# Second layer of two split experts in seven products instead of block and token form; one load and one mask moved

## The chip, the cores and the metric

The kernel runs on one core of a Trainium2 chip. The metric is the device time of one execution in microseconds (us); the median of three runs stands for a kernel. The engines are named as the profile names them: PE (TensorE, matrix products), DVE (VectorE), ACT (ScalarE), POOL (GpSimd), SP (SyncE, which only issues DMAs). SBUF is the on-chip memory, PSUM holds the output of PE in eight banks.

## The reference, cut to what matters

A recurrent attention block (RWKV-5) makes one row of 384 numbers per token, and a mixture of eight experts works on these rows. Each token goes to the one expert with the largest logit.

```
for t in range(S):                                   # 4 x 8 heads, 768 steps, 48 wide
    cur = einsum('bhd,bhe->bhde', u * k_t, v_t)
    y[:, :, t] = einsum('bhd,bhde->bhe', r_t, state + cur)
    state = w * state + einsum('bhd,bhe->bhde', k_t, v_t)
x = y reshaped to (3072 tokens, 384)
logits = x @ w_gate                                  # (3072, 8)
expert = argmax(logits);  gate = softmax(logits)[expert]
for e in range(8):
    h = maximum(x[expert == e] @ w1[e], 0)           # 384 -> 1024
    out[expert == e] = gate * (h @ w2[e])            # 1024 -> 384
```

With the reference's inputs the eight experts get 380, 348, 359, 410, 409, 389, 374 and 403 tokens. All arithmetic is float32.

## The kernel before, in words

All the work is in the function `straight`. If a count falls outside the limits that it was built for, a flag is set and a general version runs behind it (L1392 to L1395); the flag compares the count of each expert with an upper bound `caps` and a lower bound `lows` (L849, L850).

**The scan loop** (L731 to L791) has 16 turns, one for each pair of heads of each batch. Turn i, in the order of the program: `p_own(i)` (PE, L278) forms the token's own term from the product `rp` that POOL made (`pairs`, L265); `own_t` (DVE, L282) transposes it; `p_scores` (PE, L290) writes the scores of six chunks into the PSUM tiles `X`; `scale(i + 1)` (DVE, L259) prepares the next turn; `diag(i)` (ACT, L296) writes twelve diagonal blocks into A; `mask(i, 0)`, `mask(i, 1)` (DVE, L302) and `mask(i, 2)` (DVE, L304) copy the scores above the diagonal into A. `p_tr(i - 2)` (PE, L351) turns older outputs back to token rows, and `keep(i - 2)` (ACT, L356 and L357) copies these to the SBUF buffer `xb`, the second copy out of the bank that mask 2 reads too. `p_out(i - 1)` (PE, L333, L338) makes the output of the turn before, and `out_t` (ACT, L343) copies it. In turns 6, 10 and 14 the flag `rt` is set: there a finished batch is routed as well, `p_rank` (PE), `slots` (DVE, L386, L388), `gates` (DVE, L392 to L394). Rows are then sent to sorted places in the DRAM tensor `rows` by scatters of POOL (`send`, L405), one to two in a turn. The buffers `xb` are two, by batch in turns, so `keep` of one batch waits until the scatters of the batch two before have read them. Tiny POOL copies named `turn` (L743, L871) hold POOL back until a given instruction of another engine is done.

**The experts.** Experts 0 and 1 are split: their first 160 sorted rows (`early`) begin while the last batch is still at work, and the rests (`late[0]`, `late[1]`, rows 160 and up, 224 and 192 wide) follow. The other six experts, sorted by count on the chip, are `late[2]` to `late[7]`, 416 to 364 rows wide. A loop (L880 to L926) takes them in order; `o` is the expert before `p`:

- For a rest (k < 2) the first layer is `L1` (PE L470, ACT L472): per eighth of the 1024 features three products of 128x128 weights with the rows, into one bank of `hbank`. After every second eighth `result` (L869) lets POOL do one `turn` and one of ten waiting scatters of the early rows.
- For a full expert the first layer is `quarter` (L477), a seven-product scheme (PE L492, DVE L506 to L516, ACT L503, L521) on sums of weights (`quarter_sums`) and of tokens (`token_sums`), both DVE, all at the helper line L687.
- While `p`'s first layer is at work, `inner_sums` (L662, DVE, L687) makes four sums of blocks of the hidden activations `hT` of `o`, one per quarter, and behind the first layer the second layer of `o` follows.
- The second layer has two parts. `L2` (L545) takes the rows beyond the first `c` = 128 * `nt` tokens in feature-major form: 24 products with weights as the stationary operand (PE L552), then DVE transposes (L554) and block-wise scatters. `tokens_out` (L573) takes the first `c` tokens in token-major form. With `nt` = 2 these are 256 tokens in seven products of four matmuls each of 192 columns (PE L598), with DVE and ACT operations (L616, L623, L627, L631) between them and two scatters; with `nt` = 1 these are 128 tokens in eight matmuls of 384 columns into the bank `tr` (PE L585), one DVE operation (L587) and one scatter. The rests have `nt` = 1, the full experts 2.
- The seven products read `inner_sums` and eight sums of the second-layer weights (`tums`). `weight_sums` (L651) puts these eight in the list `aside`; each scatter of POOL takes one from the list and does it behind itself (L677, L678), and `rest` does what is left. For `nt` = 1 both functions return at once.

Which instruction waits for which is worked out by the framework from the order of the program. Each engine takes its own instructions in that order. SP's queue at a turn k of the expert loop: `weights1(k + 2)` (four DMAs of 384 KB into the first-layer weights, each waiting until PE has read the quarter that it replaces), in turns from k = 1 `weights2(k + 1)`, and last the rows of expert k + 2 (`load`, L450: four DMAs of 169 KB and one small).

```
689    early = [Pass(e, 0, EARLY, 0, early_bufs[e]) for e in range(2)]
690    late = [Pass(k, EARLY if k < 2 else 0, n, 1 if k < 2 else 2) for k, n in enumerate(WIDTH)]
...
916            if k == 0:
917                okay()
918            weights1(p.k + 2)
919            if k > 0:
920                p.weight_sums()
921                o.L2()
922                o.tokens_out()
923                rest()
924                weights2(o.k + 2)
925        if k + 2 < n:
926            late[k + 2].load()
```

Of the kernel before, what the change touches and what calls it, by code (L numbers as in the profile page):

```python
# [43 lines left out]
def straight(tc, rk, vk, w, w1, w2, out, flag):  # L44
# [389 lines left out]
    class Pass:  # L434
# [3 lines left out]
        def __init__(self, k, s0, n, nt, bufs=None):  # L438
            self.k, self.s0, self.n, self.nt = k, s0, n, nt
            self.c = 128 * nt  # L440
            self.e, self.last = k, []
            self.g, self.gc = -(-n // 32), self.c // 32
            if bufs:
                self.x, self.t, self.h, self.y, self.yo, self.ix = bufs
# [100 lines left out]
        def L2(self):  # L545

            n, g = self.n - self.c, self.g - self.gc
            y = self.y
            for m in range(DT):
# [23 lines left out]
        def tokens_out(self):  # L573
# [8 lines left out]

            if nt == 1:
                for f in range(FT):
                    nc.tensor.matmul(tr[:, 0:DM], lhsT=self.h[:, f, 0:128], rhs=w2s[self.k % 2][f // 2][:, f % 2, :],  # L585
                                     start=f == 0, stop=f == FT - 1, skip_group_check=True)
                nc.vector.tensor_scalar_mul(self.yt[0].rearrange("p (a m i) -> p m a i", a=HP, m=DT),  # L587
                                            tr[:, 0:DM].rearrange("p (m a i) -> p m a i", a=HP, m=DT), self.xg[:, 0, 0:1])
                scatter(out, it2[:, 0:1], self.yt[0][:, :], N)
                return  # L590

# [36 lines left out]

            product(tr, 0, A(0, 0), B_(0, 0))
            product(tr, 1, A(0, 1), B_(1, 0))  # L630
            nc.scalar.copy(so[0], tr[:, 0:Z])  # L631
            add(so[1], tr, 1, so[0])
            weigh(place(0, 0), so[1], 0)
            product(yps[0], 0, Sm(1), Tm(1))
            product(yps[0], 1, Sm(0), Tm(0))
            add(so[2], yps[0], 0, so[0])
            add(so[3], yps[0], 1, so[2])
            weigh(so[4], so[3], 0)
            weigh(so[5], so[3], 1)
            product(dsb, 0, Sm(3), B_(1, 1))  # L640
            final(0, 1, dsb, 0, so[4])
            scatter(out, it2[:, 0:1], self.yt[0][:, :], N)
            product(yps[1], 0, Sm(2), Tm(2))
            add(so[6], yps[1], 0, so[2])
            weigh(so[7], so[6], 1)
            final(1, 1, yps[1], 0, so[5])
            product(tr, 0, A(1, 1), Tm(3))
            final(1, 0, tr, 0, so[7])
            scatter(out, it2[:, 1:2], self.yt[1][:, :], N)

        def weight_sums(self):  # L651

            if self.nt < 2:
                return
            ws = w2s[self.k % 2]

            for q in range(2):
                (b11, b12), (b21, b22) = [[halves(ws[q + u])[:, :, z] for z in range(2)] for u in (0, 2)]
                t1, t2, t3, t4 = [x[:, 2 * q:2 * q + 2].rearrange("p f (m c) -> p f m c", m=DT) for x in tums[self.k % 2]]
                aside.extend([(t1, b12, b11), (t2, b22, t1), (t3, b22, b12), (t4, b21, t2)])  # L660

        def inner_sums(self, js=range(4)):  # L662

            if self.nt < 2:
                return
            h = self.h
            a11, a12, a21, a22 = [h[:, 4 * u:4 * u + 4, t * 128:(t + 1) * 128] for t in range(2) for u in range(2)]
            for j in js:
                op(sums[j], *((a21, a22, ALU.add), (sums[0], a11, ALU.subtract), (a11, a21, ALU.subtract),
                              (a12, sums[1], ALU.subtract))[j])  # L670
# [18 lines left out]
    early = [Pass(e, 0, EARLY, 0, early_bufs[e]) for e in range(2)]  # L689
    late = [Pass(k, EARLY if k < 2 else 0, n, 1 if k < 2 else 2) for k, n in enumerate(WIDTH)]  # L690

# [20 lines left out]

    nc.gpsimd.memset(lows[:, 0:2], 0.0)
    nc.gpsimd.memset(lows[:, 2:], float(PAD))
    keys(0, nc.vector)
# [15 lines left out]
    for i in range(1, U):  # L731
# [32 lines left out]
        if behind:  # L764
            p_scores(i, range(4, G))
        if 2 <= i:
            keep(i - 2)
        mask(i, 2)
        if i == U - 1:
# [105 lines left out]
    def rest():  # L875
        while aside:
            op(*aside.pop(0), ALU.subtract, nc.gpsimd)


    for k, p in enumerate(late):  # L880
# [14 lines left out]
        else:  # L895

            if k < 2:
                for f in range(FT):
                    p.L1((f,))
                    if f % 2:  # L900
                        result(p, f)
# [14 lines left out]
            if k == 0:  # L916
                okay()
            weights1(p.k + 2)
            if k > 0:
# [4 lines left out]
                weights2(o.k + 2)  # L924
        if k + 2 < n:
            late[k + 2].load()  # L926
# [517 lines left out]
```

## Time and profile before

| what | us |
|---|---|
| median of 3 runs (lowest, highest) | 371.15 (370.73, 374.41) |
| the profiled execution, its span | 372.72, 371.0 |
| PE busy | 357.9 |
| DVE busy | 247.2 |
| POOL busy | 201.8 |
| ACT busy | 138.5 |
| scan loop, PE | about 14 to 119 |
| first and second layer of the early rows, PE | to 146.0 |
| first layer of rests 0 and 1 | 146.0 to 163.0 |
| second layer of rest 0 | 163.0 to 173.5 |
| quarters of expert 2 | 173.5 to 189.0 |
| second layer of rest 1 | 189.0 to 199.5 |

The chain in the page follows the work that ended last backwards from release to release. A line of the timeline gives the start, the length, the engine, the line of the kernel, the operation with its tiles, and the number of instructions; where an engine stood idle before, brackets give how long and what released it. A float32 product is two instructions on PE. A line of 687 is a helper: there the tile tells which sum it is.

### The profile page before, as it was taken

How to read it: one execution, taken by the hardware profiler on the slowest of the kernel's cores; microseconds unless marked ns; L12 is line 12 of the kernel's file. 1: busy time of each engine (PE TensorE's matmuls, PEld its weight loads, DVE VectorE, ACT ScalarE, POOL GpSimd, SP SyncE). 2: the span in 40 equal slices, each digit the busy share in tenths (PEclk: the TensorE clock that was granted, in tenths of full speed). 3: DMA queues.
4: the chain of work that ended last, by engine and by line, in shares of the span. 5: the costliest groups of instructions: out<-in, count | busy, mean ns of one | idle time of the engine just before them, and what ended most of it. 6: DMA issues, size and time to landing. Idle time of an engine off the chain costs nothing.

```text
span 371.0 us, 9058 instructions
## 1 busy us (share of the span) xinstructions
PE 357.9 (96%) x3371; PEld 334.9 (90%) x3371; DVE 247.2 (67%) x639; ACT 138.5 (37%) x401; POOL 201.8 (54%) x236
## 2 busy tenths in 40 slices
PE   6999999999999999999999999999999999999991
PEld 6788888887889999997997999999999999999891
DVE  8787888788773325046595895697688589685531
ACT  2487878768785310320220412221230221113210
POOL 3377868979955430453116506903931951999341
PEclk9699999999999999999999999999999999999997
DMA  7995798886656883695837716823842843313401
GB/s 209 275 256 174 249 265 248 265 256 195 232 113 233 261 350 77 177 279 159 216 90 214 180 55 202 194 89 100 224 151 92 201 149 125 112 49 88 141 21 49
DMA packets 34981, 65.08 MB, mean 175 GB/s; under 512 B 18378, under 2 KB 19410, under 8 KB 34928
## 3 DMA queue, kind: packets, MB, share of 16 engines
q1 hardware_dynamic: 29392, 49.86, 48.1%
q0 software_dynamic: 3808, 9.84, 7.5%
q10 hardware_dynamic: 1728, 4.72, 3.8%
q8 instruction: 28, 0.46, 0.5%
q14 instruction: 25, 0.20, 0.2%
HBM read 53.29 MB, written 11.26 MB: 174 GB/s over the span
## 4 chain that ended last, share of the span: by engine, by line
PE 87%; DVE 3%; DMA 2%; ACT 2%; issue 2%; POOL 2%; POOLq 0%; DVEq 0%; ACTq 0%
PE X L552 12%; PE X L492 12%; PE X L470 8%; PE tr L598 6%; PE yps L598 6%; PE yps L492 5%; PE X L290 5%; PE yps L333 4%; PE tr L351 3%; PE tr L492 3%; PE dsb L492 3%; PE tr L585 3%; PE yps L338 2%; PE yps L552 2%; PE dsb L598 2%; PE dsb L313 2%
## 5 line engine op out<-in xcount | busy, mean ns | idle before, releaser
L673 POOL DMA_INDIRECT out_dram<-yo,ix x33 | 33.3, 1009 | 84.6 <-DVE ia L579 79.6
L296 ACT ACTIVATE A<-ident,own 128x128 f32<-128x128 f32 x192 | 57.9, 388 | 12.6 <-DVE own L282 11.3
L552 PE MATMUL X<-hT,w2s 128*128 128x96 f32 (+7 forms) x384 | 47.4, 283 | 0.0
L552 PEld LDWEIGHTS X<-hT,w2s 128*128 128x128 f32 x384 | 47.2, 191 | 0.2
L405 POOL DMA_INDIRECT rows<-xb,slot x24 | 33.1, 1379 | 15.5 <-issue 4.5
L290 PEld LDWEIGHTS X<-RK 48*128 48x128 f32 x384 | 23.5, 190 | 7.5 <-issue 4.9
L290 PE MATMUL X<-RK 48*128 48x128 f32 x384 | 27.6, 286 | 2.1 <-DVE RK L259 2.1
L259 DVE TENSOR_TENSOR RK<-rk,TT 112x1536 f32<-112x1536 f32 x16 | 27.6, 1725 | 0.0
L265 POOL TENSOR_TENSOR rp<-rk 112x768 f32<-112x768 f32 x15 | 27.2, 1816 | 0.0
L302 DVE COPY_PREDICATED A<-strict,X 128x512 f32<-128x512 int32 x32 | 23.1, 740 | 4.5 <-ACT A L296 4.5
L492 PE MATMUL X<-xT,w1s 128*128 128x208 f32 (+5 forms) x120 | 26.0, 331 | 0.0
L598 PE MATMUL yps<-tums,sums 128*128 128x192 f32 x144 | 25.4, 326 | 0.0
L687 POOL TENSOR_TENSOR tums<-w2s,tums 128x384 f32<-128x384 f32 x24 | 24.6, 1027 | 0.4
L333 PE MATMUL yps<-A,vk 128*48 128x128 f32 x384 | 24.0, 274 | 0.0
L598 PEld LDWEIGHTS yps<-tums,sums 128*128 128x128 f32 x144 | 23.7, 190 | 0.0
L492 PEld LDWEIGHTS X<-xT,w1s 128*128 128x128 f32 x120 | 20.9, 190 | 0.5
L333 PEld LDWEIGHTS yps<-A,vk 128*48 128x48 f32 x384 | 20.2, 123 | 0.5
L687 DVE TENSOR_TENSOR quart<-w1s 128x128 f32<-128x128 f32 x69 | 19.1, 285 | 0.0
L521 ACT ACTIVATE hT<-hT 128x416 f32<-128x416 f32 (+5 forms) x23 | 12.3, 537 | 15.6 <-DVE hT L513 15.6
L503 ACT COPY mida<-X 128x208 f32<-128x208 f32 (+5 forms) x12 | 3.9, 324 | 37.9 <-PE X L492 37.9
L351 PE MATMUL tr<-sel,yT 112*128 112x104 f32 x128 | 18.0, 284 | 0.0
L631 ACT COPY so<-tr 128x192 f32<-128x192 f32 x6 | 1.9, 318 | 43.0 <-PE tr L598 43.0
(204 smaller groups left out, 805.6 us busy)
## 6 DMA issues: line engine op xcount, KB each, us to landing
w1s<-in_w_dram SPq DMA_DIRECT2D x36, 384.0 KB, 3.2
rk<-in_rk_dram SPq DMA_DIRECT2D x16, 672.0 KB, 7.0
w2s<-in_w_dram SPq DMA_DIRECT2D x24, 384.0 KB, 3.6
vk<-in_vk_dram SPq DMA_DIRECT2D x16, 528.0 KB, 4.5
w2s<-in_w_dram ACTq DMA_DIRECT2D x8, 384.0 KB, 6.3
xs<-rows SPq DMA_DIRECT2D x16, 169.0 KB, 5.2
w1s<-in_w_dram ACTq DMA_DIRECT2D x4, 384.0 KB, 3.4
rows<-zt SPq DMA_DIRECT2D x1, 1248.0 KB, 7.0
```

The source lines that it names most:

```text
L259: nc.vector.tensor_tensor(RKs[i % 3][0:KP].rearrange("p u (c t) -> p u c t", t=C), x[0:KP].rearrange("p u (c t) -> p u c t", t=C), bc(TT[: ...
L290: nc.tensor.matmul(o, lhsT=r[q, 1, c * C:(c + 1) * C], rhs=r[q, 0, c * C:(c + 1) * C], start=True, stop=True, skip_group_check=True)
L296: nc.scalar.activation(A[:, place(c, h), :], ident, func=ACT.Copy, scale=own[i % 2][:, c, h:h + 1])
L333: nc.tensor.matmul(o(c, h), lhsT=v[:, c, h * D:(h + 1) * D], rhs=A[:, place(c, h), :], start=c < 2, stop=c == 0, skip_group_check=True)
L351: nc.tensor.matmul(trv[c // 4][:, c % 4, :], lhsT=yTs[i % 3][0:KP, c & 1, (c // 2) * C:(c // 2 + 1) * C], rhs=sel[:, c & 1, i % HP, :], st ...
L405: s_ = nc.gpsimd.indirect_dma_start(out=rows[:, :], out_offset=bass.IndirectOffsetOnAxis(ap=slot[b % 2][:, c:c + 1], axis=0), in_=xbs[b % ...
L470: nc.tensor.matmul(p[:, 0:self.n], lhsT=w1s[self.k % 2][f // 2][:, m, f % 2 * 128:(f % 2 + 1) * 128], rhs=self.t[:, m, 0:self.n], start=m ...
L492: nc.tensor.matmul(p[:, at * n:(at + 1) * n], lhsT=a, rhs=b, start=j == 0, stop=j == len(ab) - 1, skip_group_check=True)
L552: nc.tensor.matmul(p[:, 0:n], lhsT=w2s[self.k % 2][f // 2][:, f % 2, m * 128:(m + 1) * 128], rhs=self.h[:, f, self.c:self.n], start=f == 0 ...
L598: nc.tensor.matmul(p[:, at * Z:(at + 1) * Z], lhsT=a(f), rhs=b(f), start=f == 0, stop=f == FT // 2 - 1, skip_group_check=True)
L673: s_ = nc.gpsimd.indirect_dma_start(out=to[:, :], out_offset=bass.IndirectOffsetOnAxis(ap=at, axis=0), in_=x, in_offset=None, bounds_check ...
L687: (eng or nc.vector).tensor_tensor(o, a, b, op=how)
```

## The change

The rests get `nt` = 2. Their 256 tokens are more than they are wide, so `L2` returns at once (`n <= 0`), the columns of `hT` beyond the width are set to zero by two POOL memsets ahead of the loop, and the form for `nt` = 1 is removed. The weight sums of rest 0 are put in `aside` ahead of the loop, so that the scatters of the early rows do them one by one; those of rest 1 are put there in turn k = 1. The inner sums of rest 0 are made on DVE at the start of turn k = 1, those of rest 1 one per quarter of turn k = 2. Rest 1 gets another list of PSUM banks for its seven products. The rows of expert 2 are loaded ahead of `weights1(2)` in turn k = 0 instead of behind it. The lower bound on the counts of experts 0 and 1 becomes 320, as for the others. In the turns of the scan loop with `rt`, `mask(i, 2)` stands ahead of `keep(i - 2)`.

```diff
-            self.g, self.gc = -(-n // 32), self.c // 32
+            self.g = -(-n // 32)
+            self.gc = min(self.g, self.c // 32)
+            self.banks = tr, yps[0], dsb, yps[1], tr
...
         def L2(self):
             n, g = self.n - self.c, self.g - self.gc
+            if n <= 0:
+                return
...
-            if nt == 1:
-                for f in range(FT):
-                    nc.tensor.matmul(tr[:, 0:DM], lhsT=self.h[:, f, 0:128], rhs=w2s[self.k % 2][f // 2][:, f % 2, :],
-                                     start=f == 0, stop=f == FT - 1, skip_group_check=True)
-                nc.vector.tensor_scalar_mul(self.yt[0].rearrange("p (a m i) -> p m a i", a=HP, m=DT),
-                                            tr[:, 0:DM].rearrange("p (m a i) -> p m a i", a=HP, m=DT), self.xg[:, 0, 0:1])
-                scatter(out, it2[:, 0:1], self.yt[0][:, :], N)
-                return
...
+            ba, bb, bd, be, bf = self.banks
-            product(tr, 0, A(0, 0), B_(0, 0))
-            product(tr, 1, A(0, 1), B_(1, 0))
+            product(ba, 0, A(0, 0), B_(0, 0))
+            product(ba, 1, A(0, 1), B_(1, 0))
...
         def weight_sums(self):
-            if self.nt < 2:
-                return
...
         def inner_sums(self, js=range(4)):
-            if self.nt < 2:
-                return
...
-    late = [Pass(k, EARLY if k < 2 else 0, n, 1 if k < 2 else 2) for k, n in enumerate(WIDTH)]
+    late = [Pass(k, EARLY if k < 2 else 0, n, 2) for k, n in enumerate(WIDTH)]
...
-    nc.gpsimd.memset(lows[:, 0:2], 0.0)
-    nc.gpsimd.memset(lows[:, 2:], float(PAD))
+    nc.gpsimd.memset(lows, float(PAD))
...
+        if rt:
+            mask(i, 2)
         if 2 <= i:
             keep(i - 2)
-        mask(i, 2)
+        if not rt:
+            mask(i, 2)
...
+    for p in late[:2]:
+        nc.gpsimd.memset(p.h[:, :, p.n:p.c], 0.0)
+    late[1].banks = zbank[0], zbank[1], zbank[2], yps[0], dsb
...
+    late[0].weight_sums()
     for k, p in enumerate(late):
...
             if k < 2:
+                if k:
+                    o.inner_sums()
                 for f in range(FT):
...
             if k == 0:
                 okay()
+                late[2].load()
             weights1(p.k + 2)
...
-        if k + 2 < n:
+        if 0 < k < n - 2:
             late[k + 2].load()
```

More of the change, by code (lines that the diff above doesn't have):

```diff
@@ L627, in weigh @@
                 nc.scalar.activation(o, x, func=ACT.Copy, scale=g[:, t])
-            product(tr, 0, A(0, 0), B_(0, 0))
-            product(tr, 1, A(0, 1), B_(1, 0))
-            nc.scalar.copy(so[0], tr[:, 0:Z])
-            add(so[1], tr, 1, so[0])
+            ba, bb, bd, be, bf = self.banks
+            product(ba, 0, A(0, 0), B_(0, 0))
+            product(ba, 1, A(0, 1), B_(1, 0))
+            nc.scalar.copy(so[0], ba[:, 0:Z])
+            add(so[1], ba, 1, so[0])
             weigh(place(0, 0), so[1], 0)
[L634 to L637, printed above, removed]
+            product(bb, 0, Sm(1), Tm(1))
+            product(bb, 1, Sm(0), Tm(0))
+            add(so[2], bb, 0, so[0])
+            add(so[3], bb, 1, so[2])
             weigh(so[4], so[3], 0)
             weigh(so[5], so[3], 1)
-            product(dsb, 0, Sm(3), B_(1, 1))
-            final(0, 1, dsb, 0, so[4])
+            product(bd, 0, Sm(3), B_(1, 1))
+            final(0, 1, bd, 0, so[4])
             scatter(out, it2[:, 0:1], self.yt[0][:, :], N)
-            product(yps[1], 0, Sm(2), Tm(2))
-            add(so[6], yps[1], 0, so[2])
+            product(be, 0, Sm(2), Tm(2))
+            add(so[6], be, 0, so[2])
             weigh(so[7], so[6], 1)
-            final(1, 1, yps[1], 0, so[5])
-            product(tr, 0, A(1, 1), Tm(3))
-            final(1, 0, tr, 0, so[7])
+            final(1, 1, be, 0, so[5])
+            product(bf, 0, A(1, 1), Tm(3))
+            final(1, 0, bf, 0, so[7])
             scatter(out, it2[:, 1:2], self.yt[1][:, :], N)
         def weight_sums(self):
-            if self.nt < 2:
-                return
             ws = w2s[self.k % 2]
```

## The prediction, made before the changed kernel was run

> **What bounds the kernel now.** I read the page first: the busy table and the chain that ended last.
>
> ```profile
> PE 357.9 (96%) x3371; PEld 334.9 (90%) x3371; DVE 247.2 (67%) x639; ACT 138.5 (37%) x401; POOL 201.8 (54%) x236
> ...
> PE 87%; DVE 3%; DMA 2%; ACT 2%; issue 2%; POOL 2%; POOLq 0%; DVEq 0%; ACTq 0%
> ```
>
> The chain is PE nearly throughout, and from 121.9 to 363 us it has no other engine in it. The table by stretches gives PE 17.00 of 17 us in 146-163, 10.50 of 10.5 in 163-173.5, 10.50 in 189-199.5, at granted clock 1.00. So behind 122 us PE time that goes is gained, and a wait that PE gets is lost, one for one.
>
> Second, the timeline of PE alone, round the rests of experts 0 and 1 and one full expert (start, length, line, operation):
>
> ```profile
> 163.00 5.49 PE L552 MATMUL X<-hT,w2s 128*128 128x96 f32 x48
> 168.33 5.35 PE L585 MATMUL tr<-w2s,hT 128*128 128x384 f32 x16
> 173.52 1.22 PE L492 MATMUL X<-xT,w1s 128*128 128x208 f32 x6
> ...
> 188.99 5.47 PE L552 MATMUL X<-hT,w2s 128*128 128x64 f32 x48
> 194.30 5.38 PE L585 MATMUL tr<-w2s,hT 128*128 128x384 f32 x16
> 199.51 1.21 PE L492 MATMUL X<-xT,w1s 128*128 128x206 f32 x6
> ...
> 221.37 2.76 PE L598 MATMUL tr<-w2s,hT 128*128 128x192 f32 x16
> 223.97 2.76 PE L598 MATMUL yps<-tums,sums 128*128 128x192 f32 x16
> ...
> 229.16 1.46 PE L598 MATMUL tr<-tums,hT 128*128 128x192 f32 x8
> ```
>
> To be seen: the second layer of rest 0 takes 173.52 - 163.00 = 10.52 us, of rest 1 199.51 - 188.99 = 10.52 (64 columns cost what 96 do), and the seven products of a full expert, the form that both get, 230.47 - 221.37 = 9.10 (the next L492 starts at 230.47).
>
> Third, POOL's timeline, which must now deliver the weight sums, and last all engines at 80-88 us, where the one PE wait behind the start-up lies that the mask can touch.
>
> ```profile
> 160.53 0.97 POOL L673 DMA_INDIRECT out_dram<-yoe,ixe  x1 [0.21 <-issue]
> ...
> 198.35 1.03 POOL L687 TENSOR_TENSOR tums<-w2s 128x384 f32<-128x384 f32 x1
> ```
>
> ```profile
> 80.67 0.33 ACT L357 COPY xb<-X 128x208 f32<-128x208 f32 x1 [1.08 <-DMA rows<-xb,slot]
> ...
> 81.04 0.74 DVE L304 COPY_PREDICATED A<-strict,X 128x512 f32<-128x512 int32 x1 [1.34 <-ACT xb L357]
> ...
> 85.90 1.81 POOL L265 TENSOR_TENSOR rp<-rk 112x768 f32<-112x768 f32 x1
> ...
> 87.77 0.51 PE L278 MATMUL dsb<-rp,wug 112*2 112x192 f32 x8 [0.82 <-DVE A L304]
> ```
>
> **Term 1, PE in the two rests: -2.84 us.** Per rest 48 + 16 half-matmuls go, 56 (7 products x 4 x 2) come, 0.1625 us each: 10.52 - 9.10 = 1.42, twice 2.84. That the columns beyond 224 or 192 are zeros doesn't make them cheaper, so the row of full experts holds.
>
> **Term 2, the third mask: -0.82 us.** In turns 6, 10, 14 of the scan loop the mask (L304) is put ahead of the two copies `keep`. It now waits for the second copy (L357). In turn 10 that copy waits for an earlier scatter of the same buffer to land, so VectorE stands 1.34 us, and `own`, the scale (L259) and with them POOL's product rp (L265) start that much later: rp ends at 87.71, PE takes it at 87.77 after 0.82 idle. Moved, the mask starts at 79.70; rp ends near 86.4, ScalarE's diagonals (free at 81.76 from its copies, 3.62 long) at 85.4, the mask of turn 11 at 86.8; PE is free at 86.95, so all 0.82 goes, with 0.15 to spare. Next late is that mask. Turns 6 and 14: VectorE waits 0.16 in each, and the copy L357 gets a wait for the mask instead, about 0.6; behind it on ScalarE stand the output copies (0.86), done at 56.1 and 108.4, where the next diagonals start at 56.04 and 108.37: 0 to 0.1 each, and no PE row there waits for ScalarE; taken at 0. Ends for the whole term: 0 (another wait at 86.95) and -0.82; I take -0.82 because each link has a row.
>
> **Term 3, start of expert 3: +0.45 us.** Rest 1 loses its block form, which gave VectorE 5.3 us before its sums were due. Its PE products now start when the quarters of turn k=2 end (call it T). Turn k=3 shows VectorE's load there, the inner sums (0.68 x 4) included: quarters end at 214.84, sums and transposes for the next expert at 223.07, so T + 8.23. Then 0.48 of index work (224.70 to 225.18), 0.26 for the first sum, 0.75 for two more: T + 9.72 plus some 0.1 of starts. PE has left its seven products at T + 9.10, and its second product of the next quarter, at T + 9.44, writes the bank zbank[1] that those two sums read. Stall 0.4 to 0.5. The bank list with zbank first keeps the other hazards away: third bank read to T + 10.7, written from T + 10.9. Ends: 0 and 1.0 (VectorE 0.5 later, as where a sum took 1.02 instead of 0.68 at 235.43).
>
> **Term 4, rest 0 waits for sums: +0.3 us.** PE would reach it at 163.00; its sixth and eighth weight sums are due at 163.00 + 2.60 + 0.65 = 166.25 and 171.44, and bank tr must be read by 170.79. POOL: two memsets first (312 elements per partition took 0.347, 960 took 0.898; these have 256 and 512, so some 0.8), in the 15.45 us in which POOL stood before 148.90; they wait for the sends that land near 139.7. Then eight rounds of turn, scatter and sum: 0.17 + 0.21 + 0.98 + 1.02 + some 0.2 gaps = 2.57, the first 2.9, and 0.6 where the trace shows a scatter late at 159.17: the eighth ends at 148.9 + 2.9 + 7 x 2.57 + 0.6 = 170.4, the sixth near 165. No stall, 1.0 in hand. If each of five sums that meet VectorE took the longest row, 1.35, the eighth ends at 172.1: stall 0.6. VectorE: four sums from 155.68 (2.7), transposes, token and quarter sums (7.29 by 162.76 to 170.05), index work and first sum 0.8: bank tr read at 166.5, 4.3 before it is due. But now two-input sums of both engines overlap in time: VectorE's sums of hT mean 1.019 over 12 where the shortest is 0.681, that is 0.68 lost per expert, at its one meeting with POOL's sums. Some six of POOL's eight sums fall between 155.7 and 170; six meetings cost 4.1: 170.6, no stall. If each costs what the longest such row lost, 1.82 - 0.68 = 1.14, six cost 6.8: 173.3, a stall of 2.5. Ends 0 and 2.5; I take 0.3 for both engines together, near the lower end, since 1.82 is one row and the mean is of twelve.
>
> [...]
>
> **At nothing, with cover.** Expert 2's rows: five DMAs pass four weight DMAs on SP, which stood idle from 143.4 to 148.47, when PE frees the first weights; their issue takes 2.5 (155.82 to 158.36), so weights keep their time. VectorE's 7.08 wait for these rows before 162.76 goes, and PE, which needs their transposes at 172, sees nothing of it; it is the room for the sums. Left where they were, the transposes would start at 162.76 as before and bank tr be read at 170.9, with no room for any meeting. Second-layer weights wait for POOL too: the last quarter of rest 0 is free at 171 instead of 173, and is used 20 us later. ScalarE gets 5 operations per rest (2.0 us), in idle of 10.5. POOL has 3 scatters fewer and 16 sums more (16.3 us): eight as above, eight for rest 1 from about 172 to 183, due near 190. Cover gone, each would be Term 4 again. The bounds of 320 rows hold: experts 0 and 1 have 380 and 348 tokens.
>
> **Sum.** -2.84 - 0.82 + 0.45 + 0.3 = -2.9 us. The profiled execution took 372.7 (span 371.0 and 1.7 around), 1.6 over the median 371.15: it goes to 369.8, the median to 368.2.
>
> **Rivals.** (a) PE gains in the rests but another wait stands at 87 us: without Term 2, 369.1. For it: rp, mask and PE end within 0.06 there; against: all three hang on the same VectorE wait. (b) VectorE is late for bank tr by Term 4's upper end, 2.5 instead of 0.3: 370.4. For it: the 1.82 row, and quarter sums (281 to 289 ns) that so far never met POOL's; against: the mean. (c) Slower: POOL is the bound at rest 0. Eight rounds at the longest scatter (1.36), sum (1.35) and a gap of 0.58 as after each turn that waited take 3.65 each; the eighth sum ends at 178.1, a stall of 6.7 against gains of 3.2: 374.7. It decides from 3.2 us a round, when the eighth ends at 174.6. Against it: at 225-234 scatter and sum alternate at 2.2 beside a busy VectorE. (d) All stalls hidden: 371.15 - 3.66 = 367.5.
>
> **How the numbers follow.** Forecast 0.55, (a) 0.12, (b) 0.13, (c) 0.08, (d) 0.12. About 1% (3.7 us) is what a measurement tells from no change. The forecast lies at 0.8%: same. Faster by over 1%, below 367.4: half of (d) and a tail of 0.14 of the forecast by spread of the medians, 0.2. Slower by over 1%, above 374.9: most of (c), and what I don't see, 0.08. Same 0.72. Range 367.0 to 370.6: from (d) less 0.5 of spread to (b) and a little; out are (c) and tails, 2 in 10.
>
> **What would show it.** Right: PE L598 after 163 in 9.1 us per rest without waits; no 0.82 before L278 near 87; a PE gap of 0.4 at the second L492 of expert 3. Wrong: PE rows waiting for POOL tums L687 (Term 4), for DVE so L616 beyond 0.5 (Term 3), or L278 still waiting for rp.

## The result, and the profile after

The changed kernel takes 371.67 us, median of 20 runs, where the kernel before, run beside it, takes 371.2 (20 runs): ratio 1.0004, 95% interval 0.9981 to 1.0027 (the ratios in this document compare the runs and are not the quotients of the medians). One of the 20 runs of the change took 925.22 us, some 550 more than the others; no trace of it was kept, its cause is open, and the ratio leaves it out. So nothing is to be seen of the forecast 2.9 us, and the time lies above the range of 367.0 to 370.6. Run again later the change took 371.57 against 371.92, ratio 0.9986 (0.9959 to 1.0014).

The profiled execution of the change took 370.8 us with a span of 369.1. That it lies below the 372.7 of the profile before proves nothing: the clock granted to PE in the first 20 us was 0.83 in the execution before and 1.00 in this one, and turn 1 of the scan loop began at 18.05 in the one and at 15.73 in the other, which shifts all later starts. So stages are compared, each measured between starts of PE rows within one execution.

The page of the change, as before: busy times first, then the chain that ended last.

```profile
PE 353.6 (96%) x3355; PEld 334.4 (91%) x3355; DVE 266.9 (72%) x645; ACT 142.9 (39%) x411; POOL 218.0 (59%) x250
...
PE 81%; DVE 13%; issue 2%; POOL 1%; DMA 0%; ACT 0%; POOLq 0%; DVEq 0%
```

PE is busy 4.3 us less, but the chain now runs over DVE for 13% of the span where it was 3%. The timeline of PE shows where (start, length, line, operation; in brackets the idle time before the row and its releaser). L278 was L278 before, L594 was L598, L494 was L492, L612 was L616 and L680 the helper L687:

```profile
84.94 0.51 PE L278 MATMUL dsb<-rp,wug 112*2 112x192 f32 x8
...
160.01 2.76 PE L594 MATMUL tr<-w2s,hT 128*128 128x192 f32 x16
162.61 2.76 PE L594 MATMUL yps<-tums,sums 128*128 128x192 f32 x16
...
166.51 1.46 PE L594 MATMUL yps<-tums,sums 128*128 128x192 f32 x8
170.42 1.57 PE L594 MATMUL tr<-tums,hT 128*128 128x192 f32 x8 [2.44 <-DVE so L612]
171.82 1.22 PE L494 MATMUL X<-xT,w1s 128*128 128x208 f32 x6
...
187.30 2.76 PE L594 MATMUL X<-w2s,hT 128*128 128x192 f32 x16
...
197.29 1.62 PE L494 MATMUL X<-xT,w1s 128*128 128x206 f32 x6 [0.73 <-DVE so L612]
```

To be seen: the rows of the seven products have the lengths of the full experts (2.76 and 1.46), but before the last product of rest 0 PE stands 2.44 us until DVE has read bank `tr`, and after rest 1 it stands 0.73 and loses some more inside the first quarter of expert 3 (its first row is 1.62 long). Rest 0 takes 171.82 - 160.01 = 11.81 us instead of 10.52, rest 1 197.29 - 187.30 = 9.99. L278 near 85 has no wait any more.

Why DVE is late shows its own timeline. The sums of rest 0 come first, then the token and quarter sums of expert 2, last the addition that frees bank `tr`:

```profile
152.76 1.16 DVE L680 TENSOR_TENSOR sums<-hT 128x512 f32<-128x512 f32 x1
...
155.16 1.95 DVE L680 TENSOR_TENSOR sums<-hT,sums 128x512 f32<-128x512 f32 x1
...
158.55 1.04 DVE L680 TENSOR_TENSOR toks<-xT 128x208 f32<-128x208 f32 x1
...
160.21 1.95 DVE L680 TENSOR_TENSOR toks<-xT,toks 128x208 f32<-128x208 f32 x1
162.08 0.28 DVE L680 TENSOR_TENSOR quart<-w1s 128x128 f32<-128x128 f32 x1
...
162.80 1.73 DVE L680 TENSOR_TENSOR quart<-w1s,quart 128x128 f32<-128x128 f32 x1
...
165.18 1.83 DVE L680 TENSOR_TENSOR quart<-w1s 128x128 f32<-128x128 f32 x1
...
170.01 0.35 DVE L612 TENSOR_TENSOR so<-tr,so 128x192 f32<-128x192 f32 x1
...
176.87 3.05 DVE L680 TENSOR_TENSOR sums<-hT 128x512 f32<-128x512 f32 x1
```

And the weight sums in the timeline of POOL over the same time:

```profile
155.55 1.01 POOL L680 TENSOR_TENSOR tums<-w2s,tums 128x384 f32<-128x384 f32 x1
...
158.34 1.01 POOL L680 TENSOR_TENSOR tums<-w2s 128x384 f32<-128x384 f32 x1
...
160.90 1.01 POOL L680 TENSOR_TENSOR tums<-w2s,tums 128x384 f32<-128x384 f32 x1
...
163.37 1.01 POOL L680 TENSOR_TENSOR tums<-w2s,w2s 128x384 f32<-128x384 f32 x1
...
165.84 1.01 POOL L680 TENSOR_TENSOR tums<-w2s,tums 128x384 f32<-128x384 f32 x1
...
176.41 1.01 POOL L680 TENSOR_TENSOR tums<-w2s,w2s 128x384 f32<-128x384 f32 x1
177.38 1.01 POOL L680 TENSOR_TENSOR tums<-w2s,tums 128x384 f32<-128x384 f32 x1
```

Each long row of DVE lies over a row of POOL, and no other two-input row of this stretch is long. With 0.68, 0.37 and 0.28 as the lengths of a sum, a token sum and a quarter sum that met nothing, the six rows from 152.76 to 165.18 lost 0.48, 1.27, 0.67, 1.58, 1.45 and 1.55: 7.0 us. POOL's sums stay at 1.01; only its small copies `turn` between them grow, up to 0.65 where the kernel before has at most 0.19, and its eighth sum ends at 166.85, in time. Without the 7.0 us DVE would have been done with its first reading of bank `tr` near 163.4, where PE wants it at 167.81.

The account in stages (us, starts of PE rows):

| stage | before | after |
|---|---|---|
| second layer of rest 0 | 10.52 | 11.81 |
| quarters of expert 2 | 15.47 | 15.48 |
| second layer of rest 1 | 10.52 | 9.99 |
| expert 3's quarters and expert 2's second layer | 30.96 | 31.51 |
| first layer of rest 0 to start of expert 4 | 84.46 | 85.78 |
| own-term products, turn 11 to 12 | 7.44 | 6.55 |
| own-term products, turn 6 to 15 | 58.94 | 57.93 |

The mask gained 0.9 to 1.0 in its stretch, the rests lost 1.3: +0.3 to +0.4. The medians say +0.5, but the interval of the ratio holds no change as well.

### The profile page after: what moved, and what is told of

Its sections match the earlier page's. It is cut to its first block, busy times and chain, and to the rows that moved or that the text cites. A ratio compares the mean times of both kernels' runs of the same rounds, so it can differ in the third digit from the quotient of the medians.

```text
span 369.1 us, 9067 instructions
## 1 busy us (share of the span) xinstructions
PE 353.6 (96%) x3355; PEld 334.4 (91%) x3355; DVE 266.9 (72%) x645; ACT 142.9 (39%) x411; POOL 218.0 (59%) x250
## 4 chain that ended last, share of the span: by engine, by line
PE 81%; DVE 13%; issue 2%; POOL 1%; DMA 0%; ACT 0%; POOLq 0%; DVEq 0%
PE X L494 11%; PE X L556 10%; PE tr L594 7%; PE yps L594 6%; PE X L472 6%; PE X L290 6%; PE yps L333 6%; PE tr L351 5%; PE yps L494 4%; PE yps L338 3%; DVE quart L680 3%; PE tr L494 2%; PE dsb L494 2%; PE yps L556 2%; PE dsb L313 2%; PE dsb L594 2%
## 5 line engine op out<-in xcount | busy, mean ns | idle before, releaser
L666 POOL DMA_INDIRECT out_dram<-yo,ix x28 | 28.6, 1022 | 66.8 <-DVE ia L583 62.5
L405 POOL DMA_INDIRECT rows<-xb,slot x24 | 30.4, 1265 | 13.0 <-issue 4.8
L556 PE MATMUL X<-hT,w2s 128*128 128x160 f32 (+5 forms) x288 | 36.5, 287 | 0.0
L556 PEld LDWEIGHTS X<-hT,w2s 128*128 128x128 f32 x288 | 36.2, 191 | 0.2
L680 POOL TENSOR_TENSOR tums<-w2s,tums 128x384 f32<-128x384 f32 x32 | 33.1, 1033 | 0.6
L594 PE MATMUL yps<-tums,sums 128*128 128x192 f32 x176 | 31.1, 326 | 0.0
L666 POOL DMA_INDIRECT out_dram<-yt,it x16 | 16.7, 1046 | 20.9 <-DVE so L612 16.2
L594 PEld LDWEIGHTS yps<-tums,sums 128*128 128x128 f32 x176 | 29.0, 190 | 0.0
L494 PE MATMUL X<-xT,w1s 128*128 128x208 f32 (+5 forms) x120 | 26.4, 332 | 0.8 <-DVE so L612 0.7
L333 PE MATMUL yps<-A,vk 128*48 128x128 f32 x384 | 24.0, 274 | 0.0
L680 DVE TENSOR_TENSOR sums<-hT 128x512 f32<-128x512 f32 x16 | 20.7, 1293 | 3.2 <-ACT hT L474 3.2
L494 PEld LDWEIGHTS X<-xT,w1s 128*128 128x128 f32 x120 | 20.8, 190 | 1.4 <-DVE so L612 1.4
L333 PEld LDWEIGHTS yps<-A,vk 128*48 128x48 f32 x384 | 20.3, 123 | 0.5
L680 DVE TENSOR_TENSOR quart<-w1s 128x128 f32<-128x128 f32 x69 | 20.6, 306 | 0.0
L594 PE MATMUL tr<-w2s,hT 128*128 128x192 f32 x112 | 19.4, 326 | 0.0
```

Source lines behind the costliest of these rows:

```text
L333: nc.tensor.matmul(o(c, h), lhsT=v[:, c, h * D:(h + 1) * D], rhs=A[:, place(c, h), :], start=c < 2, stop=c == 0, skip_group_check=True)
L405: s_ = nc.gpsimd.indirect_dma_start(out=rows[:, :], out_offset=bass.IndirectOffsetOnAxis(ap=slot[b % 2][:, c:c + 1], axis=0), in_=xbs[b % ...
L494: nc.tensor.matmul(p[:, at * n:(at + 1) * n], lhsT=a, rhs=b, start=j == 0, stop=j == len(ab) - 1, skip_group_check=True)
L556: nc.tensor.matmul(p[:, 0:n], lhsT=w2s[self.k % 2][f // 2][:, f % 2, m * 128:(m + 1) * 128], rhs=self.h[:, f, self.c:self.n], start=f == 0 ...
L594: nc.tensor.matmul(p[:, at * Z:(at + 1) * Z], lhsT=a(f), rhs=b(f), start=f == 0, stop=f == FT // 2 - 1, skip_group_check=True)
L666: s_ = nc.gpsimd.indirect_dma_start(out=to[:, :], out_offset=bass.IndirectOffsetOnAxis(ap=at, axis=0), in_=x, in_offset=None, bounds_check ...
```

## The experiments

GpSimd is POOL in the rows, VectorE DVE. The theory after the result: PE's products cost what the prediction says and the mask saves what it says; all that is missing is VectorE held by GpSimd's weight sums, at about twice the assumed price. Where a VectorE operation and a sum of GpSimd run beside one another the text speaks of a meeting, of a full one if the whole sum lies within the VectorE row. Rivals: VectorE's own list is too long with or without GpSimd; any work of GpSimd on SBUF holds it; the mask gains nothing in time. "Stage" below is the stretch from rest 0's first layer to the start of expert 4.

**First: the mask alone, and the rests alone.** The one is the kernel before with

```
+        if rt:
+            mask(i, 2)
         if 2 <= i:
             keep(i - 2)
-        mask(i, 2)
+        if not rt:
+            mask(i, 2)
```

and the other is the change with these lines as they were.

> The kernel before with nothing but the third mask moved ahead of the copies in the three turns with ranks. Theory (the mask's gain is real and the rests of the two experts cost it again): PE's wait of 0.82 us before the own-term product of turn 12 is gone, the time falls by 0.8 to 1.0, to about 370.3 beside 371.2. Rival (the mask gains nothing, PE meets another wait there, and the lead that the changed kernel shows behind turn 12 comes from its start): 371.2, with a wait of 0.5 or more left at that place.

> The changed kernel with the third mask put back behind the copies: the rests in seven products and the moved load alone. Theory: the rests together lose 1.3 us against before (rest 0 takes 11.8 instead of 10.5, rest 1 with the start of expert 3 about 10.4), so 372.3 to 372.7 beside 371.2. Rival (the rests gain and something else, such as the start, spends it): below 370.5.

Measured: mask alone 376.02 us against 376.12 of the kernel before on this chip (a slower one: the first four kernels ran on it), ratio 1.0000 (0.9964 to 1.0037), stage 84.45; the interval from turn 11 to 12 is 6.55, so the wait is gone, but the time settles nothing. (Its profile is of an execution of 380.45 us, so only stages and intervals are read from it.) The rests alone took 379.4, ratio 1.0085 (1.0045 to 1.0126), so they are a loss of about 3 us, more than the 1.3 that the change's profile shows for them; rest 0 took 12.76 us and the stage 86.52, 2.1 more than in the kernel before. The timeline of PE in the rests alone says what came on top:

```profile
178.37 2.52 PE L594 MATMUL tr<-tums,hT 128*128 128x192 f32 x8 [2.48 <-DVE so L612]
180.69 1.98 PE L494 MATMUL X<-xT,w1s 128*128 128x208 f32 x6
```

The wait is the same as in the change, 2.48 against 2.44, but the rows behind it are longer, 2.52 instead of 1.46 and 1.98 instead of 1.22. The same kernel by stretches (busy time of each engine, then the granted PE clock, DMA share, GB/s):

```profile
178.30:180.70 2.40, 2.33 (x9) 2.33 (x10) 1.65 (x6) 1.71 (x4) 0.51 (x1) 0.61 1.27 170
180.70:182.50 1.80, 1.80 (x7) 1.74 (x7) 0.42 (x1) 0.33 (x1) 1.60 (x3) 0.57 1.01 198
```

In these two stretches behind the wait, 4.2 us together, PE was granted 0.61 and 0.57 of its clock. That is a second price of the same wait; the change's own profile has 1.00 there. It is taken up again below.

**Second: GpSimd's sums taken out of VectorE's way.** In the change, the eight weight sums of rest 0 are done ahead of the expert loop, all at once, while VectorE has few two-input operations to do:

```
     late[0].weight_sums()
+    rest()
```

A further kernel does the same with both rests (`for p in late[:2]: p.weight_sums()`, then `rest()`, and `if k > 1` ahead of `p.weight_sums()` in the loop).

> The changed kernel, with the eight weight sums of rest 0 done by POOL at once ahead of the loop, while VectorE and POOL stand idle, instead of one behind each scatter. All of VectorE's work in that stretch stays. Theory (each operation of VectorE with two SBUF inputs that meets a POOL sum is held for 1.3 to 1.6 us, and five to six such meetings make bank tr late): the long rows of 1.0 to 1.95 us are gone from the token and quarter sums, VectorE reads bank tr near 3 + 163 us of the span instead of 170, PE waits 0 to 0.3 instead of 2.4 in rest 0, rest 0 takes 9.1 to 9.4, and the time is 368.9 to 369.3. Rival (VectorE simply has too much to do there): the wait stays above 1.8 and the time above 371. Second rival (the sums are late for PE): as the first theory in time, but PE waits now for POOL in the profile of the changed kernel, which it did not.

> As the kernel with rest 0's weight sums ahead of the loop, and the eight of rest 1 behind them, all sixteen before the first scatter of the early rows. Theory of the meetings: the first inner sum of rest 1, 3.05 us in the changed kernel, falls to 0.7, VectorE is free 8.2 instead of 9.2 us after the quarters of expert 2, PE's loss at the start of expert 3 falls from 1.3 to 0.4 or 0.5, and the time is 368.1 to 368.6. Rival (the load of VectorE): no change against the kernel with the first eight alone. Rival (POOL is now the bound, since its scatters start up to 8 us later): PE or VectorE waits for a scatter's buffer, time above 369.5.

Measured: first sums early 373.66 us, ratio 0.9927 (0.9897 to 0.9957); both early 373.56, ratio 0.9956 (0.9921 to 0.9991). One line turns no gain into one of 2.5 us by medians. In the timeline of PE of the kernel with the first sums early, the rest has the predicted form:

```profile
167.91 2.76 PE L594 MATMUL tr<-w2s,hT 128*128 128x192 f32 x16
...
174.41 1.46 PE L594 MATMUL yps<-tums,sums 128*128 128x192 f32 x8
175.71 1.46 PE L594 MATMUL tr<-tums,hT 128*128 128x192 f32 x8
```

Both rests take 9.10 us, the stage 82.09 with the first sums early and 82.14 with both. The first is 2.37 less than before, which is 2.84 less 0.46 in the quarters of expert 3: 0.36 in the first quarter, at the place that the prediction names, and 0.10 at the start of the last. With both early no sum of rest 1 meets anything (four rows of 0.68), and the 0.36 stays. So this part doesn't come from meetings: it is VectorE's own list, done 8.21 us after the quarters of expert 2 end (8.22 with the first early). The 0.10 stays too. Its likely cause is VectorE's first sum in expert 3's quarters, which takes 4.0 to 4.1 us beside GpSimd's sums in both kernels and 1.75 in the kernel before.

**Third: is it GpSimd's reading, or GpSimd at work?** In the change, each weight sum of rest 0 becomes three memsets of the same tile:

```
+    aside[:] = [(t, None, None) for t, _, _ in aside]
...
+        if a is None:
+            for _ in range(3):
+                nc.gpsimd.memset(t, 0.0)
```

> The change with GpSimd's eight weight sums of rest 0 replaced, in place, by three memsets of the same tile each (the sums are left out, so the rows of expert 0's rest are not what the reference has; the instructions on PE, VectorE and ScalarE are as many as in the change). The memset of 128x256 took 0.39 us in the change, so a round takes about 1.1 to 1.2 us against 1.01 of a sum: GpSimd is as busy as before, at the same places, but reads nothing from SBUF. Theory: a VectorE operation with two SBUF inputs is held by a GpSimd operation that reads SBUF. Then VectorE's sums and quart sums beside these rounds fall from 1.7 to 1.95 us back to 0.3 to 0.7, and the second layer of rest 0 takes 9.1 to 9.5 us instead of 11.8, the stage from rest 0's first layer to expert 4 82.5 to 83.4 instead of 85.8. Rival 1: any GpSimd operation on SBUF holds VectorE: 11.3 to 12.3 us, as in the change. Rival 2: VectorE's own list between rest 0's first layer and bank tr is too long, with GpSimd or without: 11 us or more, with VectorE's rows at their short durations.

Measured (one profile): rest 0 10.00 us, stage 83.07. First the timeline of VectorE, then that of GpSimd, in this kernel:

```profile
162.56 0.28 DVE L688 TENSOR_TENSOR quart<-w1s,quart 128x128 f32<-128x128 f32 x1
...
165.79 0.36 DVE L612 TENSOR_TENSOR so<-tr,so 128x192 f32<-128x192 f32 x1
```

```profile
158.87 1.39 POOL L677 MEMSET tums<- 128x384 f32 x3
...
162.17 1.39 POOL L677 MEMSET tums<- 128x384 f32 x3
```

GpSimd is busy longer than with the sums (1.39 against 1.01 a round), writes the same tiles and issues the same scatters, yet no VectorE row beside them is long: the quarter sum at 162.56, in the middle of the memsets that begin at 162.17, takes 0.28. Bank `tr` is read as soon as PE has written it. Both rivals fall: it is not VectorE's list, and not any work of GpSimd, but its sums, which read SBUF where the memsets only write. Rest 0 lies 0.5 us above the expected 9.5 because GpSimd is late here: with the longer rounds PE waits 0.43 for the sixth `tums`, and its last row, which needs the eighth, is 1.66 long instead of 1.46.

**Fourth: the length of GpSimd's operation.** In the change, only the first half of each weight sum of rest 0 is made (128x192), the other half is set to zero ahead of the loop:

```
-                aside.extend([(t1, b12, b11), (t2, b22, t1), (t3, b22, b12), (t4, b21, t2)])
+                new = [(t1, b12, b11), (t2, b22, t1), (t3, b22, b12), (t4, b21, t2)]
+                aside.extend([tuple(x[:, 0:1] for x in y) for y in new] if self.k == 0 else new)
```

> The change with the eight weight sums of rest 0 cut to their first half, 128x192 instead of 128x384 (the other half is set to zero ahead of the loop, in GpSimd's idle time; the rows of expert 0's rest are not what the reference has). GpSimd's row falls from 1.01 to an estimated 0.5 us, and as many of VectorE's two-input operations meet one. In the change each of the meetings behind 155 us lost VectorE 1.27 to 1.58 us, 0.3 to 0.6 more than GpSimd's row is long. Theory: VectorE is held for GpSimd's row and 0.3 to 0.6 us around it: the loss falls to 0.8 to 1.1 per meeting, VectorE reads bank tr 2.0 to 2.6 us earlier, the second layer of rest 0 takes 9.1 to 9.9 us instead of 11.8. Rival: the price of a meeting is fixed, whatever GpSimd's length: 11.5 to 11.8 us. Second rival: it goes with the length alone: a loss of 0.6 to 0.8, 9.1 to 9.3 us.

Measured (one profile): rest 0 9.10 us. VectorE and GpSimd in this kernel:

```profile
154.44 1.55 DVE L681 TENSOR_TENSOR sums<-hT,sums 128x512 f32<-128x512 f32 x1
...
160.78 1.34 DVE L681 TENSOR_TENSOR quart<-w1s 128x128 f32<-128x128 f32 x2
...
164.76 0.48 DVE L681 TENSOR_TENSOR quart<-w1s 128x128 f32<-128x128 f32 x2
```

```profile
154.83 0.60 POOL L681 TENSOR_TENSOR tums<-w2s,tums 128x192 f32<-128x192 f32 x1
...
161.35 0.61 POOL L681 TENSOR_TENSOR tums<-w2s,w2s 128x192 f32<-128x192 f32 x1
```

A full meeting costs 1.55 - 0.68 = 0.87 and 1.34 - 0.48 = 0.86 with a row of 0.60 to 0.61, where it cost 1.27 to 1.58 with a row of 1.01. So the price follows the length of GpSimd's row and lies some 0.26 above it here, 0.26 to 0.57 in the change: the rival of a fixed price falls, and so does that of the length alone. In all VectorE loses 3.8 us instead of 7.0 and comes to bank `tr` 3.25 us earlier, more than the expected 2.0 to 2.6. The excess seems to lie partly ahead of the row (the profile's spans on POOL are rough): in the change the token sum that began at 160.21 needs 0.37 and could have ended 0.3 before GpSimd's row began at 160.90, yet it was held to 162.16, a little past that row's end.

**Fifth: the load moved back, and the rest of Term 3.** The one kernel is the change with the load of expert 2's rows behind the weights again (`if k + 2 < n` at the loop's end). The other has the first sums early and makes expert 3's quarter sums one quarter earlier:

```
+                    if k == 2 and q:
+                        late[3].quarter_sums(q - 1)
-                    if q > 1:
+                    elif q > 1:
                         late[k + 1].quarter_sums(q - 2)
```

> The change with the load of expert 2's sorted rows put back behind the weights' load (that one part undone). Theory: VectorE's transposes of these rows then wait for the transfer, and as they stand ahead of bank tr's first addition on VectorE, the second layer of rest 0 takes 13.5 to 15 us instead of 11.8, the stage to expert 4 about 87.5 to 89. Rival: the rows arrive in time all the same, since VectorE is held by the meetings with GpSimd so long that it comes to the transposes late: 11.8 us and 85.8, and the move was worth nothing in the change.

> The kernel with the first sums put ahead of the first expert (which had taken 82.09 us from rest 0's first layer to expert 4, with 0.46 us lost at expert 3's start) and one more edit: expert 3's quarter sums are each made one quarter of expert 2 earlier, so that VectorE has one set of five (1.1 us) less to do between expert 2's last quarter and bank X's first addition of rest 1. Theory: expert 3's first quarter on PE waited for VectorE's readings of bank X; VectorE comes to them 0.8 to 1.1 us earlier, the 0.46 is gone: stage 81.6 us, time 3.0 to 3.4 us below the kernel before. Rival: the set moved into quarter 1 delays VectorE there, where a sum already meets GpSimd's, and PE waits for a bank in quarter 3 instead: 82.1 us or more, time as with the first sums early alone (-2.7).

Measured: with the load moved back (one profile) rest 0 takes 13.91 us and the stage 87.20, because VectorE's transposes wait for the rows, and PE for VectorE:

```profile
159.77 1.60 DVE L463 STREAM_TRANSPOSE xT<-xs 128x416 f32<-128x416 f32 x3 [2.26 <-DMA xs<-rows]
```

```profile
171.60 2.93 PE L594 MATMUL tr<-tums,hT 128*128 128x192 f32 x8 [3.22 <-DVE so L612]
```

So the move of the load was worth 2.1 us of rest 0 in the change: 0.8 of wait (3.22 against 2.44), the rest a longer PE row (2.93 against 1.57) behind it, at a granted clock of 0.50. The slow clock is not the load's alone: the change's second profile (below) has it too, and against that one the move is worth 2.0 us in rest 0 but only 0.75 in the stage (87.20 against 86.45; 1.4 against the first). The prediction's text on cover had said that without the move there is no room for any meeting; so it is.

The other kernel took 367.2 us, ratio 0.9861 (0.9820 to 0.9901), stage 81.62. VectorE comes to rest 1's first addition 7.89 us after the quarters' end instead of 8.63, and expert 3 begins without a gap (timeline of PE):

```profile
192.95 1.46 PE L594 MATMUL dsb<-tums,hT 128*128 128x192 f32 x8
194.25 1.21 PE L494 MATMUL X<-xT,w1s 128*128 128x206 f32 x6
```

The set that moved into quarter 1 delays VectorE there, but no PE row waits for it. This version is faster than the kernel before, and than the change (below).

**Sixth: the mask on top, and all on one chip.** The kernel with the first sums early but the mask in its old place, and then mask alone, the change and the best version once more, beside one another.

> The kernel with the first sums put ahead of the first expert, but the third mask where it was before. It prices the mask on top of repaired rests. Theory: the stage from rest 0's first layer to expert 4 stays at 82.1 us, PE's interval between the own-term products of turns 11 and 12 is 7.44 us again instead of 6.55, and the time is 0.5 to 0.9 us above that with the mask moved: about -1.8 to -2.2 us to the kernel before. Rival: the mask's gain in turn 12 is given back in turns 8 and 12 (0.34 and 0.36 us longer intervals there): the time is within 0.2 us of that with the mask moved, about -2.6.

> The kernel before with the third mask moved alone, once more beside the others on one chip, since its time against the kernel before was left open within 0.4% either way. Theory (the gain at turn 12 carries through): PE's interval between the own-term products of turns 11 and 12 is 6.55 instead of 7.44 us, the time 0.5 to 0.9 us below the kernel before. Rival: turns 6 to 8 and 12 to 13 give it back: within 0.2 us of the kernel before.

> The change as it is, on the chip of the others, for the difference to the next. Its stage from rest 0's first layer to expert 4 is 1.3 us longer than in the kernel before (85.8 against 84.5), the mask saves 0.9: +0.4 us to the kernel before, and 4.1 us above the kernel with the first sums early and the third quarter's sums early. Rival, by the other run of such a kernel (the two rests alone were 3.2 us above the kernel before): +2 us or more.

> The kernel with the first sums early and the third quarter's sums early, on the chip of the others. By the stages (81.6 against 84.5 us, and 0.7 to 0.9 of the mask) it lies 3.5 to 3.8 us below the kernel before, a ratio of 0.990. Rival: the 0.986 of its first run holds, 5 us: then something ahead of the rests gains 1.3 us as well, and the stretches of the two profiles up to 146 us must show it.

| kernel | us | ratio to before | stage | turn 11 to 12 |
|---|---|---|---|---|
| first sums early, mask in its old place | 370.33 | 0.9927 (0.9891 to 0.9964) | 82.10 | 8.00 |
| mask alone, again | 370.81 | 0.9982 (0.9956 to 1.0008) | 84.46 | 6.80 |
| the change, again | 371.57 | 0.9986 (0.9959 to 1.0014) | 86.45 | 6.56 |
| best version, again | 367.28 | 0.9879 (0.9831 to 0.9928) | 81.61 | 6.56 |

In the kernel with the mask in its old place the wait is back, in PE's timeline:

```profile
86.19 0.51 PE L278 MATMUL dsb<-rp,wug 112*2 112x192 f32 x8 [1.07 <-DVE A L304]
```

The wait is 0.82 us in the kernel before and 1.07 here, both with the old place, and none of the eleven profiles with the mask moved has it. The rests alone, old place too, have none at turn 12 either, but two of 0.59 and 0.64 at turns 10 and 11, for `S` (L318, DVE). And in three kernels of that first chip with the mask moved, the mask alone among them, a wait of 0.42 to 0.45 for `S` stands at turn 13; the intervals from turn 8 to 9 and 12 to 13 are 0.34 to 0.39 longer there than in the kernel before, so most of the 0.89 is given back. In three others (the mask alone again, the load moved back, the first run of the best version) the interval from turn 11 to 12 is 6.73 to 7.25 instead of 6.55, and another wait has come: the copy L357 waits for the older scatter as before, behind it ScalarE copies `yT`, and PE's L351 needs that. With the load moved back it shows in ScalarE's and PE's timelines:

```profile
79.40 0.33 ACT L357 COPY xb<-X 128x208 f32<-128x208 f32 x1 [2.04 <-DMA rows<-xb,slot]
```

```profile
80.17 1.29 PE L351 MATMUL tr<-sel,yT 112*128 112x104 f32 x8 [0.47 <-ACT yT L343]
```

Whether the gain reaches the end, the times don't settle. The mask alone is 1.1 us below the kernel before by medians, with an interval that holds no change. With the first sums early the ratio is 0.9927 with the mask moved (first chip) and 0.9927 without (here): nothing is seen of the expected 0.5 to 0.9, though the intervals are 0.3 to 0.4% wide either way. The stretch from turn 6 to 15, first chip apart, takes 57.92 to 59.15 us in eight profiles with the mask moved (58.4 on the mean), 58.94 and 59.58 in two without. Much of this spread is turn 6, which takes 6.61 to 7.84 us in the eleven profiles with the mask moved and 6.61 to 6.76 in the three without: in three of the eleven PE stands 0.25 to 0.96 us before its last product at L333, with no releaser in the profile. Whether the move causes this is open.

The best version lies 4.6 to 5.8 us below the kernel before by medians in its two runs. Its stage gains 2.84 and the mask 0.9, 3.7 together, a ratio of 0.990, which both intervals hold (the first at its edge); what the larger medians add is not shown to be more than scatter. The change lies 4.3 us above it (expected 4.1), and 0.35 below the kernel before where +0.4 was expected, inside its interval.

In the change's second profile the stage was 86.45, not 85.78, though rest 1 took 9.09. Here too PE's clock fell behind the wait:

```profile
169.96 1.72 PE L594 MATMUL tr<-tums,hT 128*128 128x192 f32 x8 [2.46 <-DVE so L612]
171.48 2.28 PE L494 MATMUL X<-xT,w1s 128*128 128x208 f32 x6
```

```profile
170.00:171.50 1.50, 1.50 (x9) 1.50 (x10) 0.94 (x4) 1.20 (x3) 0.00 (x0) 0.91 1.30 218
171.50:173.50 2.00, 2.00 (x7) 1.93 (x6) 1.01 (x4) 0.79 (x2) 1.68 (x2) 0.50 0.93 159
```

## Why the prediction was wrong, term by term

**Term 1 (PE in the rests) was right.** Expected -2.84, 9.10 us a rest; measured 9.09 to 9.12 in every rest that did not wait, in ten of the runs above.

**Term 2 (the mask) was right in its place.** Expected -0.82: the wait at L278 went, and the interval from turn 11 to 12 fell by 0.89. How much of this reaches the time is not settled: other profiles show other waits in turns 6 to 13 (rival (a) in part). In turn 6 the copy L357 waits 0.82 us for the mask, where 0.6 was expected.

**Term 3 (start of expert 3) was right for an undisturbed VectorE.** Expected +0.45, with VectorE's list done 8.23 us after the quarters' end; with the first sums early that was 8.22, and the loss at the place named 0.36. That the whole loss was 0.46 is luck: the other 0.10 arose at the start of the last quarter. In the change's profile the list was done after 9.17 and the loss 0.89 in rest 1 and 0.55 behind it, 1.44, over the upper end of 1.0. The row of 3.05 us at 176.87 accounts for it: it met weight sums standing back to back and was held by several. With the first sums early the row in its place took 1.39, and VectorE stood 0.7 to 0.8 for PE behind it; the 3.05 uses this slack up and leaves 0.95. In the change's second profile the row took 1.35, and rest 1 9.09. The third term so failed by the same step as the fourth.

**Term 4 (rest 0 waits for sums) is the step that failed.** The prediction took +0.3, near the lower end, "since 1.82 is one row and the mean is of twelve". It had the number of meetings right, six. Its price of a meeting was the 0.68 us per expert that VectorE's sums of `hT` were seen to lose; the six lost 7.0 us, 1.17 each, and the four full ones 1.27 to 1.58. The upper end, six times 1.14, gave 6.8 us and a stall of 2.5; measured were 7.0 and, with the row behind it, 2.71. The mechanism, the place and the upper end were right; the choice between the ends was wrong.

Two faults stand behind that choice. The mean of twelve rows held many that met nothing. In the kernel before seven of the twelve take 0.68 to 0.69 and five 1.02 to 1.82, on the mean 0.81 too long; the longest is not alone (timeline of VectorE):

```profile
204.52 1.75 DVE L687 TENSOR_TENSOR sums<-hT 128x512 f32<-128x512 f32 x1
...
295.82 1.56 DVE L687 TENSOR_TENSOR sums<-hT 128x512 f32<-128x512 f32 x1
...
322.05 1.82 DVE L687 TENSOR_TENSOR sums<-hT 128x512 f32<-128x512 f32 x1
```

In the change VectorE has two-input work without a break from 158.5 to 169.6 us, so every sum of GpSimd that starts there finds one to hold, and the fitting row was the longest. And 0.68 was less than the 1.02 that one GpSimd sum takes, where the full meetings of the change cost 1.27 to 1.58, more than a whole one.

The runs show it in kind: sums that read SBUF hold VectorE (1.27 to 1.58 per full meeting), memsets that only write don't (a quarter sum amid them takes 0.28), and a row six tenths as long, 0.60 to 0.61 instead of 1.01, costs 0.86 or 0.87, some six tenths of the price.

**What was not in the sum:** that a wait of PE may cost more than itself. In the second profile of the change, in the rests alone and with the load moved back, the clock granted to PE fell to 0.50 to 0.61 for 3 to 4 us behind the wait; the quarters of expert 2 took 17.05, 16.24 and 15.77 us instead of 15.47. In the first profile, with a wait of 2.44, it stayed at 1.00; what decides between the two is not shown.

Rival (b), Term 4 at its upper end, came nearest: 370.4 against 371.7, short mainly by Term 3's loss to the same cause (1.44 where 0.45 was taken). Rivals (a), (c) and (d) fell in the change's profile: the mask's wait went and no other came near 87 us, GpSimd was in time with its eighth sum (166.85), and the stalls were not hidden.

## What to carry to other kernels

When sums that read SBUF go to GpSimd, price each by what it takes from VectorE: where VectorE had operations with two SBUF inputs without a break, a GpSimd sum that lay wholly within one of them cost it here its full length (1.01 or 0.60 us) and 0.26 to 0.57 us more, and a mean over rows that mostly met nothing hides that. Where the work can be done at any time, put it where VectorE has none of these operations to do: here one line that moved eight sums ahead of the loop took 3.7 us off the stage. A wait of PE of 2.4 to 3.2 us is to be counted with a possible slow stretch behind it: three of the four here had one, at a granted clock of 0.50 to 0.61.

## What the runs showed of the hardware

- VectorE's sums of two SBUF inputs lose 1.27 to 1.58 us to a GpSimd sum of 1.01 that lies within them, and 0.86 or 0.87 to one of 0.60. GpSimd's rows mostly keep their length (1.01) beside them, so the loss is nearly one-sided. Memsets of GpSimd, three in 1.39 us, lengthened no such row. Nor did sums of GpSimd that stood from 175.44 on in the change lengthen VectorE's operations with one input in PSUM: `hT<-X,midv` at 175.60 took 0.59 and `midx<-X,midu` at 176.10 took 0.36, as in the kernel before.
- A VectorE sum that meets GpSimd sums standing back to back can be held by several: 3.05 and 4.06 us in the change, and 4.02 in the kernel with the first sums early, for a sum that takes 0.68 alone.
- PE's granted clock fell to 0.50 to 0.61 behind waits of 2.46, 2.48 and 3.22 us, and stayed at 1.00 behind one of 2.44; what decides between the two is not shown.
